# Capped attention and a gated MLP on one core: all four output projections after the gate stages, as seven block products for two batches at a time

## The chip, the cores and the metric

The kernel runs on one core of a Trainium2 chip. The metric is the device time of one execution in microseconds (us), as the median of several runs. The core has a matrix engine (PE, which multiplies a 128-row weight tile with up to 512 columns), and four others that compute or move data: DVE, ACT, POOL and SP. In this kernel SP issues nearly all transfers between DRAM and the on-chip memory SBUF; PE's results land in eight banks of PSUM.

## The reference

```python
# q, k, v: 4 batches x 12 heads x 448 positions x 64
scores = matmul(q, k.T) / sqrt(64)
scores = cap * tanh(scores / cap)              # cap = 30
scores = scores - max(scores, axis=-1)
attn = exp(scores)
attn = attn / (sum(attn, axis=-1) + 1e-9)
x = matmul(attn, v)                            # laid out as 1792 tokens x 768
g = x @ w_gate                                 # 768 -> 1536
val = x @ w_val                                # 768 -> 1536
return (g * sigmoid(g) * val) @ w_out          # 1536 -> 768
```

All of it is fp32. The 1792 tokens are 4 batches of 448.

## The kernel before

Every large product of fp32 operands is made of three products of a shorter format, fp32r: an operand is cast to fp32r (the high part, `wh`, `xh`), and the remainder, the operand less its high part, is kept as a second tile (`wl`, `xl`). High x high, low x high and high x low are added in PSUM (L924 to L926). So one block of 128 weight rows, 128 outputs and 448 columns costs three matmuls; an **atom** is two such blocks, six matmuls.

**Attention** works in pairs of heads; batch g has six pairs, u = 6g to 6g+5. A pair's scores are computed in four tiles of 112 keys (`qk`, L730, bank `sc`), tanh and exp follow on ACT (`t`, L737 and L740), DVE adds the four tiles (`total`, L744), PE multiplies with the values (`av`, L760), and a matmul against ones gives the denominators (`sm`). These come in two forms. In the two-tile form (L777) the sums are spread over 64 rows, 448 columns, and one reciprocal of 128x448 follows (L797). In the four-tile form (`spread`, L771), used in five pairs of batch 1, the sums lie on 32 rows each and 224 columns, the reciprocal is 128x224 (L783), and the result goes through DRAM (a small store and a load) to be spread over the rows. Then `x` = `av` x reciprocal (L801).

**Stages.** The head (to about 70 us) is the attention of batch 0, with the weights' first loads and their narrowing: each weight arrives as 64-bit pairs, is cut to fp32 (`wf`), and stored to DRAM for the later batches. Then follow, on PE: the gate stage of batch 0 (72 atoms, tiles k = 0 to 11, each with a gate half and a value half), between whose atoms the pairs of batch 1 stand; the output projection of batch 0 (k = 12 to 17, 36 atoms, from the gated features `hx`, kept in SBUF as high and low parts); the gate stage of batch 1 (k = 18 to 29), with the twelve pairs of batches 2 and 3; the output projection of batch 1; the **window**, the gate stage of batches 2 and 3 together; and their output projection. The last two stages use a 2x2 block scheme with seven block products instead of eight: tokens and weights are split in two halves each, sums and differences of blocks are formed on DVE (`blocks`, `comb`, `combos`), cast into the tiles `X1` to `X7`, and seven products p = 1 to 7 (the table `PROD`) are added in banks `b1` to `b3`. The window has 12 steps of seven products (`step`, L459 to L461), the outputs three times seven (`outs`, L637 to L639).

**What sets the order.** The class `Plan` is a list scheduler that runs when the kernel is built. Each piece of work is an operation with a priority (a planned time), the engines that may do it with an assumed duration, the operations that it needs and the buffers that it takes (`BUFS` gives their number). It places operation after operation, chooses an engine where several are allowed, and the resulting static order is emitted. `join` glues parts to one operation of PE: the value product, the sums and the first half of the next pair's scores. Pools of SBUF and PSUM are opened where their first tile is taken; by `TAKES` a pool takes over the room of another, and then waits until that is closed: `X` (all seven kinds) that of the attention pool `A`, `R` (`xr`, the attention results of batches 2 and 3) that of the narrowing pool `W`, `C` (`cc`, copies of PSUM banks) that of `R`.

In the gate stages, each weight half (128 x 768) is loaded, cast (`wH`, on ACT, DVE or POOL), and its remainder subtracted (`wL`, on DVE or POOL):

```python
op(("wL", k, half), tw - LEAD['wL'] * dt, {"POOL": 2.04, "DVE": 0.95}, wL, [("wH", k, half)], [("wl", atoms[-1:])])
```

Of the kernel before, what the change touches and what calls it, by code (L numbers as in the profile page):

```python
# [16 lines left out]
P = 128  # L17
C = 112
S = 448
B = 4  # L20
# [19 lines left out]
PACE = 26.0  # L40
# [5 lines left out]
JOIN = 7  # L46

# [3 lines left out]
    xr=12, X1=3, X2=3, X3=3, X4=3, X5=3, X6=3, X7=3, cc=7, hh=3, ss=3, b1=2, b2=2, b3=2,  # L51
    rq=2, rk=2, qh=1, ql=1, kh=1, kl=1, rv=2, t=8, s=2, r1=1, r=2, x32=2, xh=7, xl=7,
    w64=3, lo=2, wf=5, wh=4, wl=4, th=2, hx=12, o=2, sc=2, av=1, sm=1, mm=2,
# [5 lines left out]
    A="rq rk qh ql kh kl rv t r1 r x32 xh xl", X="X1 X2 X3 X4 X5 X6 X7", W="w64 lo", R="xr", C="cc hh",  # L59
    att="sc av sm", win="b1 b2 b3", sb="wf wh wl th hx o ss", mm="mm", total="s",  # L60
)
POOL_OF = {tag: name for name, tags in POOLS.items() for tag in tags.split()}
TAKES = {"X": "A", "R": "W", "C": "R", "win": "att"}


class Plan:
# [14 lines left out]
    def __init__(self, bufs):  # L81
        self.bufs = bufs
        self.ops = {}
        self.alias = {}

# [5 lines left out]
    def join(self, parts, save):  # L91

        head = self.ops[parts[0]]
        rest = [self.ops.pop(k) for k in parts[1:]]
        (engine, us), = head["where"].items()
        fns = [head["fn"]] + [o["fn"] for o in rest]
        head["where"] = {engine: us + sum(o["where"][engine] for o in rest) - save}
        head["fn"] = lambda e: [f(e) for f in fns]
        for o in rest:
            head["deps"] += o["deps"]  # L100
            head["alloc"] += o["alloc"]
        for k in parts[1:]:
            self.alias[k] = parts[0]

    def run(self):
# [8 lines left out]
        for o in ops.values():  # L114
            deps = [self.alias.get(d, d) for d in o["deps"]]
            o["deps"] = [d for d in dict.fromkeys(deps) if d != o["key"]]
            o["alloc"] = [(t, [self.alias.get(r, r) for r in rs]) for t, rs in o["alloc"]]
        users, nleft = {}, {}
        for k, o in ops.items():
            o["deps"] = [d for d in o["deps"] if d is not None]  # L120
            nleft[k] = len(o["deps"])
            for d in o["deps"]:
                users.setdefault(d, []).append(k)
# [13 lines left out]
        ready = {}  # L137

# [25 lines left out]
        alone = {"rec", "x", "ga", "va", "ov"}  # L164

        def shares(k, e):
            return e == "POOL" or e == "DVE" and k[0] not in alone
# [5 lines left out]
        while ready:  # L173
# [29 lines left out]
            else:  # L203
                free[e] = s + d
                end[k] = s + d
                if shares(k, e):
                    port = max(port, s + d)
            eng[k] = e
            for tag, readers in o["alloc"]:
# [15 lines left out]
def tile_capped_attention_gated_mlp(ctx: ExitStack, tc: tile.TileContext, qd, kd, vd, cap, eye, w1, w2, out):  # L225
# [7 lines left out]
    def pool(tag):  # L233
        name = POOL_OF[tag]
        if name not in opened:
# [4 lines left out]
            side = "right" if name in ("W", "R", "C", "att", "win") else "left"  # L240
# [3 lines left out]
    for tag in ("wf", "t", "w64", "mm", "sc"):  # L244
        pool(tag)
# [22 lines left out]


# [6 lines left out]
    total = [const.tile([P, 2, S], F32, name=f"total{i}") for i in range(BUFS["s"])]  # L276
# [30 lines left out]
    gcols = [S] * B  # L307
    GROUPS = [[(g, 0, NJ)] for g in range(B)]
    NG = B
# [9 lines left out]
    t += 0.5 * PAIR  # L319
    for g in range(2):  # L320
        L1, L2 = 72 * mm_us + 7.0 * (4 if g == 0 else 12), 36 * mm_us + 7.0 * (2 if g == 0 else 0)
        for a in range(108):
            z, L = (a / 72, L1) if a < 72 else ((a - 72) / 36, L2)
            atom_at[18 * g + a // 6, a % 6] = t + (L1 if a >= 72 else 0.0) + L * z
            atom_len[18 * g + a // 6, a % 6] = L / (72 if a < 72 else 36)
        if g == 0:
            for c in range(NCC):
                pair_at[NCC + c] = t + 2.0 + PACE * c
            for c in range(2 * NCC):
                pair_at[2 * NCC + c] = t + L1 + L2 - 4.0 + (72 * mm_us + 7.0 * 12 + 4.0) / (2 * NCC) * c  # L330
        else:
            split_at = t + L1 + 8.0
            combo_at = t + 0.5 * L1
        t += L1 + L2
    win_at = [t + 10.6 * mm_us * f for f in range(NFC)]
    t += 10.6 * mm_us * NFC
# [15 lines left out]
    for c in range(HALF):  # L352
        RAW[2, c] = [("XL", "B11", c), ("T1", c)]
        RAW[3, c] = [("XL", "T1", c)]
        RAW[2, c + HALF] = [("XL", "B21", c), ("T4", c)]
        RAW[3, c + HALF] = [("XL", "B22", c), ("T3", c), ("T2", c)]

    def blocks():
        def raw(z, c):
            return {  # L360
                "B11": ("x32", 2 * NCC + c), "B21": ("x32", 2 * NCC + c + HALF), "B12": ("x32", 3 * NCC + c),
                "B22": ("x32", 3 * NCC + c + HALF), "T1": ("x32", 3 * NCC + c),
            }.get(z, (z, c))

        def diff(e, z, a, b, c):
            if z != "T1":
# [3 lines left out]
        for c in range(HALF):  # L370
            t0 = split_at + 14.0 * c
            x = [("x", 2 * NCC + c), ("x", 2 * NCC + c + HALF), ("x", 3 * NCC + c), ("x", 3 * NCC + c + HALF)]
            n = 0
            for z, a, b, deps in (
                ("T3", "B22", "B12", x), ("T1", "B12", "B11", x + [("T3", c)]), ("T2", "B22", "T1", [("T1", c)]), ("T4", "B21", "T2", [("T2", c)]),
# [3 lines left out]
                   [("ss", users)] if z != "T1" else [])  # L379
                n += 1.5  # L380
        for n, z in enumerate(BLOCKS):
            p = next(p for p in PROD if PROD[p][3] == z)
            for c in range(HALF):
# [10 lines left out]
                order = split_at + 14.0 * c + 1.5 * n  # L394
# [4 lines left out]
    def step(f):  # L399
# [30 lines left out]
        def wL(e, n):  # L430
            T["wl", "w", f, n] = st([P, 6, P], F32R, "wl")[:, : 6 if n < 3 else 3]
            sub(e, T["wl", "w", f, n], source(n), T["wh", "w", f, n])

# [9 lines left out]
        for n in range(4):  # L443
# [4 lines left out]
            op(key("wL", n), tw + 1.0, {"DVE": 0.95 * k, "POOL": 2.04 * k}, lambda e, n=n: wL(e, n), [key("wH", n)], [("wl", [("p", f, last[n])])])  # L448
# [17 lines left out]
        prev = ("p", f - 1, 4) if f else ("mm", 35, 5)  # L466
# [6 lines left out]
        def keep(e, name, bank):  # L473
            T["cc", f, name] = st([P, S], F32, "cc")
# [7 lines left out]
        op(("c1", f), t0 + dt, both, lambda e: keep(e, 0, "b2"), [("p", f, 1)], [("cc", [("ga", "w", f, 0)])])  # L482
        op(("c11", f), t0 + 2 * dt, {"DVE": 0.62}, lambda e: plus(0, "b1"), [("p", f, 2), ("c1", f)])
        op(("cu", f), t0 + 3 * dt, both, lambda e: keep(e, 1, "b2"), [("p", f, 6)], [("cc", [("ga", "w", f, 1)])])
# [651 lines left out]
```

## Time and profile before

| | |
|---|---|
| median of 3 runs | 695.65 us (695.4 to 696.19) |
| the profiled execution | 696.79 us, of which the span of its instructions is 695.0 |
| busy: PE, DVE, ACT, POOL | 676.9 (97%), 566.7 (82%), 376.7 (54%), 100.8 us (14%) |
| mean DMA rate | 155 GB/s |

The span goes from the first to the last instruction of the execution; what lies around it is start and end of the program. Busy time counts what an engine computes, not its waiting or its issuing of transfers. PE's weight loads are a row of their own (PEld) and run beside its matmuls. The durations of matmuls overlap in the profile, so that their sum says less than their starts. A group of instructions is named by line, engine, operation and tiles: `mm<-hx,wl` is a matmul into `mm` from `hx` and `wl`.

### The profile page before, as it was taken

The numbers are of one execution on the slowest core, as the hardware profiler recorded it, in microseconds if no ns is written. First come the engines' busy times: TensorE is split into PE (matmuls) and PEld (weight loads), VectorE is DVE, ScalarE is ACT, GpSimd is POOL, SyncE is SP. The second block draws the span as 40 slices with busy tenths as digits, with TensorE's granted clock in tenths as the row PEclk, the third lists the DMA queues.
The fourth block names the chain that finished last, engine by engine and source line by source line (L and its number), as shares of the span: only waits on it lengthen the run. The fifth ranks groups of instructions, "written<-read, shape, count | busy, mean of one in ns | idle before, by whom it ended". The sixth has DMA issues, their size and how long they took to land.

```text
span 695.0 us, 9189 instructions
## 1 busy us (share of the span) xinstructions
PE 676.9 (97%) x3424; PEld 524.7 (75%) x3424; DVE 566.7 (82%) x694; ACT 376.7 (54%) x513; POOL 100.8 (14%) x86
## 2 busy tenths in 40 slices
PE   7889999999999999999999999999999999999996
PEld 2223787867867877777666777989999999989995
DVE  4999998999989577797997976988788798899740
ACT  6989667686765455454554653743433333474310
POOL 1312201021131022022220101002112111110000
PEclk9999999999999999999999999999999999999999
DMA  8655677896887533346784212131212212135311
GB/s 286 216 174 194 215 261 265 250 308 236 263 279 250 169 106 110 96 155 235 232 306 157 88 58 82 64 127 46 91 45 59 79 45 70 47 115 174 114 66 58
DMA packets 42652, 107.62 MB, mean 155 GB/s; under 512 B 4692, under 2 KB 19944, under 8 KB 42600
## 3 DMA queue, kind: packets, MB, share of 16 engines
q1 hardware_dynamic: 42312, 106.73, 46.4%
q8 instruction: 29, 0.48, 0.3%
q10 hardware_dynamic: 288, 0.23, 0.1%
q14 instruction: 23, 0.19, 0.1%
HBM read 82.54 MB, written 24.40 MB: 154 GB/s over the span
## 4 chain that ended last, share of the span: by engine, by line
PE 89%; DVE 6%; ACT 3%; DMA 1%; issue 0%; ACTq 0%; DVEq 0%
PE mm L924 14%; PE mm L925 13%; PE mm L926 13%; PE av L760 9%; PE sc L730 8%; PE b L459 7%; PE b L460 7%; PE b L461 7%; PE b L639 3%; PE b L638 3%; PE b L637 3%; DVE total L744 2%; PE sm L777 2%; ACT t L737 1%; DVE r L797 1%; ACT t L740 1%
## 5 line engine op out<-in xcount | busy, mean ns | idle before, releaser
L737 ACT ACTIVATE t<-sc 112x896 f32<-112x896 f32 x96 | 83.3, 917 | 71.2 <-PE sc L730 71.0
L267 DVE TENSOR_TENSOR wl<-wf,wh 128x768 fp32r<-128x768 f32 (+1 forms) x104 | 104.2, 1009 | 5.5 <-ACT wh L258 4.4
L924 PE MATMUL mm<-xh,wh 128*128 128x448 f32 x288 | 108.4, 377 | 0.0
L925 PE MATMUL mm<-xh,wl 128*128 128x448 f32 x288 | 105.3, 366 | 0.0
L926 PE MATMUL mm<-xl,wh 128*128 128x448 f32 x288 | 105.3, 365 | 0.0
L258 ACT ACTIVATE wh<-wf 128x768 fp32r<-128x768 f32 (+1 forms) x86 | 68.7, 799 | 64.7 <-PE b L639 14.7
L459 PE MATMUL b<-X,wh 128*128 128x448 f32 x252 | 92.2, 366 | 1.4 <-ACT cc L258 1.4
L460 PE MATMUL b<-X,wl 128*128 128x448 f32 x252 | 92.1, 365 | 0.0
L461 PE MATMUL b<-X,wh 128*128 128x448 f32 x252 | 92.1, 365 | 0.0
L740 ACT ACTIVATE t<-t 112x896 f32<-112x896 f32 x96 | 86.7, 955 | 0.1
L760 PE MATMUL av<-t,rv 112*64 112x448 f32 x384 | 77.5, 545 | 4.5 <-DVE x L801 4.3
L797 DVE RECIPROCAL r<-sm 128x448 f32<-128x448 f32 x19 | 56.2, 2956 | 24.2 <-PE sm L777 24.2
L924 PEld LDWEIGHTS mm<-xh,wh 128*128 128x128 f32 x288 | 54.1, 188 | 17.1 <-issue 11.9
L760 PEld LDWEIGHTS av<-t,rv 112*64 112x64 f32 x384 | 25.4, 136 | 48.1 <-issue 37.2
L926 PEld LDWEIGHTS mm<-xl,wh 128*128 128x128 f32 x288 | 54.1, 188 | 4.3
L925 PEld LDWEIGHTS mm<-xh,wl 128*128 128x128 f32 x288 | 54.2, 188 | 4.0 <-DVE wl L267 0.2
L744 DVE TENSOR_TENSOR total<-total,t 112x896 f32<-112x896 f32 x47 | 53.7, 1143 | 2.3 <-ACT t L740 2.1
L924 PE MATMUL mm<-hx,wh 128*128 128x448 f32 x144 | 53.7, 373 | 0.0
L926 PE MATMUL mm<-hx,wh 128*128 128x448 f32 x144 | 52.8, 366 | 0.0
L925 PE MATMUL mm<-hx,wl 128*128 128x448 f32 x144 | 52.7, 366 | 0.0
L459 PEld LDWEIGHTS b<-X,wh 128*128 128x128 f32 x252 | 47.4, 188 | 5.5 <-ACT cc L258 1.8
L461 PEld LDWEIGHTS b<-X,wh 128*128 128x128 f32 x252 | 47.4, 188 | 3.7
(121 smaller groups left out, 1164.7 us busy)
## 6 DMA issues: line engine op xcount, KB each, us to landing
wf<-w SPq DMA_DIRECT2D x81, 384.0 KB, 3.2
w<-w SPq DMA_DIRECT2D x36, 768.0 KB, 5.7
w<-wf SPq DMA_DIRECT2D x36, 384.0 KB, 4.1
rq<-qd SPq DMA_DIRECT2D x24, 224.0 KB, 4.5
rv<-vd SPq DMA_DIRECT2D x24, 224.0 KB, 3.1
rk<-kd SPq DMA_DIRECT2D x23, 224.0 KB, 4.7
w_S<-wf SPq DMA_DIRECT2D x12, 384.0 KB, 2.8
wf<-w_S SPq DMA_DIRECT2D x12, 384.0 KB, 3.2
```

The costliest lines, as they stand in the source:

```text
L258: nc.scalar.activation(out_, in_, AF.Copy, scale=1.0 if scale is None else scale)
L267: ENG[e].tensor_tensor(out_, a, b, op=ALU.subtract)
L459: nc.tensor.matmul(o, lhsT=wh, rhs=xh, start=first, stop=False, skip_group_check=True)
L460: nc.tensor.matmul(o, lhsT=wl, rhs=xh, start=False, stop=False, skip_group_check=True)
L461: nc.tensor.matmul(o, lhsT=wh, rhs=xl, start=False, stop=end, skip_group_check=True)
L737: nc.scalar.activation(T["t", u, j], T["sc", u, j][:C, :, :S], AF.Tanh, scale=icapr)
L740: nc.scalar.activation(T["t", u, j], T["t", u, j], AF.Exp, scale=capr)
L744: ENG[e].tensor_tensor(z, T["t", u, 0] if j == 1 else z, T["t", u, j], op=ALU.add)
L760: nc.tensor.matmul(T["av", u][D * i : D * i + D, :S], lhsT=T["rv", u][:C, i, j * D : j * D + D], rhs=T["t", u, j][:, i], start=j == 0, sto ...
L924: nc.tensor.matmul(o, lhsT=wh, rhs=xh, start=beg, stop=False)
L925: nc.tensor.matmul(o, lhsT=wl, rhs=xh, start=False, stop=False)
L926: nc.tensor.matmul(o, lhsT=wh, rhs=xl, start=False, stop=fin)
```

## The change

- **Outputs.** The two output projections of batches 0 and 1 (k = 12 to 17 and 30 to 35) are gone from their places. The gated features of these batches are stored to DRAM by SP (`hst`, 24 stores of 224 KB), and after the outputs of batches 2 and 3 (`outs(0)`) those of batches 0 and 1 follow in the same seven-product form (`outs(1)`), 378 matmuls where there were 432. Their features are loaded back (`hld`, 12 loads), planned 40 us ahead, into four slot kinds `H11` to `H22`, which batches 2 and 3 have used before. The w_out weights are loaded and cast a second time for `outs(1)`.
- **Narrowing of w_out** (12 halves) moves from batch 0's output stage into batch 1's gate stage, one tile every 20 us.
- **Denominators.** Pairs 6 to 22, without 11, use the four-tile form; they hold `av` in a copy in SBUF (`xk`, on ACT or DVE), which frees the bank, and multiply that copy in place when the reciprocals have come back.
- **Scores ahead.** For the pairs in `EARLY` the first half of the next pair's scores stands several products before the value product of the current one, and the second half directly before it, joined with it. The pairs of batches 2 and 3 run in the order c, c+3 of batch 2, then of batch 3 (`SEQ`).
- **Weight remainders.** For twelve halves of batch 1's gate stage (`FAR_1`: the gate halves of k = 18 to 29) the remainder is made otherwise: ACT writes -`wh` into `wl`, and a transfer issued by POOL adds `wf` to it in SBUF (`add_far`).
- **Pools.** Only `X3`, `X4`, `X5` take the attention pool's room; `X1`, `X2`, `X6`, `X7` take that of the narrowing; `cc`, `o` and `hx` are gone (`xr` tiles serve for the first two), `xr` is open from the start, `wf` has six buffers, `th` four, and the difference `T4` is made in place.

```diff
+FAR_1 = {(k, 0) for k in range(18, 30)}
+NARROW = 20.0
+GATES = {5,11,23}
+SPREAD = set(range(6,24)) - GATES
+HELD = set(range(6,24)) - GATES
+SEQ = list(range(2 * NCC)) + [NCC * g + c + h for c in range(NCC // 2) for g in (2, 3) for h in (0, NCC // 2)]
+NEXT = {u: z for u, z in zip(SEQ, SEQ[1:])}
+EARLY = set(SEQ[JOIN + 1 :]) - {2 * NCC}
-    A="rq rk qh ql kh kl rv t r1 r x32 xh xl", X="X1 X2 X3 X4 X5 X6 X7", W="w64 lo", R="xr", C="cc hh",
+    A="rq rk qh ql kh kl rv t r1 r x32 xh xl", X="X3 X4 X5", R="xr", W="w64 lo", Y="X1 X2 X6 X7", H="H11 H21 H12 H22 hh",
-TAKES = {"X": "A", "R": "W", "C": "R", "win": "att"}
+TAKES = {"X": "A", "Y": "W", "win": "att"}
...
+    def add_far(out_, in_):
+        flat = lambda z: z.rearrange("p a b -> p (a b)") if len(z.shape) == 3 else z
+        nc.gpsimd.dma_start(flat(out_), flat(in_), accum_op=ALU.add)
+
+    def rest(key, at, far, deps, fin, source, width=6, lead=5.0):
...
+        if not far:
+            op(("wL",) + key, at, {"POOL": 2.04 * k, "DVE": 0.95 * k}, lambda e: sub(e, new(), source(), T[("wh",) + key]), deps, [("wl", fin)])
+            return
+        op(("wN",) + key, at - lead, {"ACT": 0.85 * k}, lambda e: copy(e, new(), T[("wh",) + key], -1.0), deps, [("wl", fin)])
+        op(("wA",) + key, at - lead + 0.1, {"POOL": 0.86}, lambda e: add_far(T[("wl",) + key], source()), [("wN",) + key])
...
+    def outs(pr):
+        base = out_at + pr * len(OUT_ORDER) * 3 * mm_us
+        batches = (2, 3) if pr == 0 else (0, 1)
...
+        def hload(e, i, b, c):
+            T["h", pr, c + HALF * i, b] = st([P, 2, S], F32, f"H{i + 1}{b + 1}")
+            nc.sync.dma_start(T["h", pr, c + HALF * i, b], scratch["h", batches[b], c + HALF * i])
...
+                    op(("hld", i, b, c), base - 40.0 + 4.0 * i + 6.0 * b + c, {"SP": 1.28}, lambda e, i=i, b=b, c=c: hload(e, i, b, c),
+                       [("hst", g, z), ("hst", g, z + 1)], [hslot(pr, i, b, c)])
...
+            z = t0 + 3.8 * (j // 2)
+            if u in EARLY:
+                z = t0 - AHEAD if j < 2 else t0
...
+        def keep(e):
+            T["x32", u] = st([P, S], F32, "xr" if g else "x32")
+            copy(e, T["x32", u], T["av", u][:, :S])
...
-            op(("wL", k, half), tw - LEAD['wL'] * dt, {"POOL": 2.04, "DVE": 0.95}, wL, [("wH", k, half)], [("wl", atoms[-1:])])
+            rest((k, half), tw - LEAD['wL'] * dt, (k, half) in FAR_1, [("wH", k, half)], atoms[-1:], lambda half=half: T["wf", k, half])
...
+        def hst(e):
+            if i % 2 == 0:
+                scratch["h", g, i // 2] = dram.tile([P, 2, S], F32, name=f"hidden_{g}_{i // 2}")
+            nc.sync.dma_start(scratch["h", g, i // 2][:, i % 2], T["th", k])
...
-    outs()
+    outs(0)
+    outs(1)
     for u in range(JOIN, NU):
-        plan.join([("av", u), ("sum", u)] + ([("qk", u + 1, 0), ("qk", u + 1, 1)] if (u + 1) % NCC else []), 0.2)
+        nxt = NEXT.get(u)
+        if u in GATES:
+            plan.join([("av", u), ("sum", u)], 0.2)
+        elif nxt in EARLY:
+            plan.join([("qk", nxt, 2), ("qk", nxt, 3), ("av", u), ("sum", u)], 0.2, pair_at[nxt])
+            plan.join([("qk", nxt, 0), ("qk", nxt, 1)], 0.0)
+        else:
+            plan.join([("av", u), ("sum", u), ("qk", nxt, 0), ("qk", nxt, 1)], 0.2)
```

How the order changes is shown at three places. First PE, in the middle of batch 1's gate stage, around one attention pair; before:

```order
L926 MATMUL mm<-xl,wh 128x448
L760 MATMUL av<-t,rv 64x448 x8
L777 MATMUL sm<-total_81,ones 64x448 x2
L730 MATMUL sc<-qh,kl 112x448 x2
L730 MATMUL sc<-qh,kh 112x448 x2
L730 MATMUL sc<-ql,kh 112x448 x2
...
L924 MATMUL mm<-xh,wh 128x448
```

And now:

```order
L989 MATMUL mm<-xl,wh 128x448
L790 MATMUL sc<-qh,kl 112x448 x2
L790 MATMUL sc<-qh,kh 112x448 x2
L790 MATMUL sc<-ql,kh 112x448 x2
...
L822 MATMUL av<-t,rv 64x448 x8
L833 MATMUL sm<-total_85,ones 32x224 x4
L987 MATMUL mm<-xh,wh 128x448
```

The value product was followed by the sums and by the first two score tiles of the next pair; now the last two score tiles of the next pair stand directly before it, and the sums have the four-tile form.

Second ACT, around the window's first product, whose result stands in bank `b2` (`cc` or `xr` receives its copy). Before:

```order
L258 ACTIVATE wh_4081<-ss_4057 128x768
L258 ACTIVATE X5_4093<-xr_3513 128x448
L258 ACTIVATE o_4118<-mm_4040 128x448
L258 ACTIVATE wh_4122<-wf_3752 128x384
L258 ACTIVATE X6_4126<-ss_4120 128x448
L258 ACTIVATE wh_4143<-wf_4090 128x768
L258 ACTIVATE cc_4152<-b2_4108 128x448
```

And now:

```order
L1002 ACTIVATE th_3490<-mm_3448 128x448
L284 ACTIVATE X5_3531<-xr_2245 128x448
L284 ACTIVATE X5_3536<-xr_2766 128x448
L284 ACTIVATE X5_3539<-xr_3270 128x448
L284 ACTIVATE X3_3553<-xr_2383 128x448
L284 ACTIVATE X3_3556<-xr_2913 128x448
L284 ACTIVATE X3_3558<-xr_3368 128x448
L284 ACTIVATE xr_3561<-b2_3515 128x448
```

The copy of the first product stood behind a weight cast; now six casts into `X5` and `X3` stand directly before it, and those behind it follow.

Third POOL, in batch 1's gate stage, where `DMA wl<-wf` is an accumulating transfer. Before:

```order
L267 TENSOR_TENSOR wl<-wf,wh 128x768
L260 TENSOR_SCALAR wf<-w_1769 128x768
L267 TENSOR_TENSOR ql<-rq,qh 128x448
L267 TENSOR_TENSOR wl<-wf,wh 128x768
L260 TENSOR_SCALAR wh<-wf 128x768 x2
```

And now:

```order
L293 TENSOR_TENSOR kl<-rk,kh 128x448
L297 DMA wl<-wf 128x768
L286 TENSOR_SCALAR wh<-wf 128x768
L297 DMA wl<-wf 128x768
L286 TENSOR_SCALAR qh<-rq 128x448
L286 TENSOR_SCALAR wf<-w_1578 128x768
L297 DMA wl<-wf 128x768
L286 TENSOR_SCALAR qh<-rq 128x448
L804 TENSOR_TENSOR total_85<-total_85,t 112x896
L286 TENSOR_SCALAR wf<-w_1853 128x768
L297 DMA wl<-wf 128x768
```

POOL's own subtractions of weights have given way to casts, issued transfers and sums of score tiles.

## Rows read from the trace of the kernel before

**Rows 1.** The page: its head, the engines, the granted clock in 40 slices.

```profile
span 695.0 us, 9189 instructions
...
PE 676.9 (97%) x3424; PEld 524.7 (75%) x3424; DVE 566.7 (82%) x694; ACT 376.7 (54%) x513; POOL 100.8 (14%) x86
...
PEclk9999999999999999999999999999999999999999
```

**Rows 2.** Table by stage: length, busy PE, PEld, DVE, ACT, POOL, clock, DMA share, GB/s.

```profile
0.00:70.00 70.00, 59.84 (x274) 21.48 (x276) 60.23 (x64) 58.54 (x72) 15.24 (x16) 1.00 0.64 218
70.00:188.00 118.00, 118.00 (x596) 92.61 (x593) 109.48 (x138) 84.20 (x111) 16.24 (x12) 1.00 0.76 257
...
243.00:402.00 159.00, 159.00 (x874) 112.49 (x872) 131.92 (x148) 86.29 (x112) 29.90 (x27) 1.00 0.50 162
...
458.00:611.00 153.00, 151.59 (x749) 140.21 (x748) 126.70 (x178) 60.81 (x100) 27.46 (x23) 1.00 0.23 72
611.00:688.70 77.70, 77.44 (x375) 69.92 (x373) 51.90 (x59) 28.94 (x39) 1.32 (x1) 1.00 0.32 106
```

**Rows 3.** Waits of PE: us in total, times, longest us.

```profile
PE av L760 <- DVE x L801: 4.3, 4, 1.5
...
PE b L459 <- ACT cc L258: 1.4, 1, 1.4
...
PE mm L638 <- DVE wl L267: 0.3, 1, 0.3
```

**Rows 4.** The page's groups: busy us, mean ns; an output product of batches 0, 1.

```profile
L925 PE MATMUL mm<-hx,wl 128*128 128x448 f32 x144 | 52.7, 366 | 0.0
```

**Rows 5.** Timeline of PE: start us, length us; window stage, then last outputs.

```profile
500.11 0.36 PE L459 MATMUL b<-X,wh 128*128 128x448 f32 x1
...
502.54 0.36 PE L459 MATMUL b<-X,wh 128*128 128x448 f32 x1
...
685.47 0.37 PE L637 MATMUL b<-X,wh 128*128 128x448 f32 x1
...
688.37 0.37 PE L639 MATMUL b<-X,wh 128*128 128x448 f32 x1
```

**Rows 6.** Chain of waits: start us, length us; a four-tile and a two-tile pair.

```profile
113.59 3.16 PE av L760 x16
...
117.26 1.69 PE sc L730 x8
118.95 0.40 PE mm L924
119.35 0.20 PE mm L925
...
264.97 3.16 PE av L760 x16
...
268.88 1.40 PE sc L730 x12
```

**Rows 7.** Timeline of ACT at the window's start; then a group of it.

```profile
459.15 0.84 ACT L258 ACTIVATE wh<-wf 128x768 fp32r<-128x768 f32 x1 [2.30 <-issue]
459.90 0.53 ACT L258 ACTIVATE cc<-b 128x448 f32<-128x448 f32 x1
...
L258 ACT ACTIVATE X<-xr 128x448 fp32r<-128x448 f32 x12 | 6.4, 565 | 0.5 <-DVE xr L801 0.5
```

**Rows 8.** Groups of DVE by form: busy us, mean ns.

```profile
L797 DVE RECIPROCAL r<-sm 128x448 f32<-128x448 f32 x19 | 56.2, 2956 | 24.2 <-PE sm L777 24.2
...
L267 DVE TENSOR_TENSOR X<-hx,X 128x896 fp32r<-128x896 f32 x18 | 19.2, 1086 | 0.0
...
L783 DVE RECIPROCAL r<-sm 128x224 f32<-128x224 f32 x5 | 7.7, 1549 | 0.0
```

**Rows 9.** The page's DMA issues: KB each, us to landing.

```profile
wf<-w SPq DMA_DIRECT2D x81, 384.0 KB, 3.2
```

**Rows 10.** Timeline of ACT: the last copy of the kernel.

```profile
688.82 0.54 ACT L258 ACTIVATE o<-b 128x448 f32<-128x448 f32 x1 [3.22 <-PE b L639]
```

More of the change, by code (lines that the diff above doesn't have):

```diff
@@ L89, in op, with join @@
         self.ops[key] = dict(key=key, prio=prio + self.SHIFT.get(key[0], 0.0), where=where, fn=fn, deps=list(deps), alloc=list(alloc))
[L91 to L103, printed above, removed]
+    def join(self, parts, save, prio=None):
+        ops = [self.ops.pop(k) for k in parts]
+        key = ("join",) + parts[0]
+        (engine, _), = ops[0]["where"].items()
+        at = 0.0
+        for o in ops:
+            at += o["where"][engine]
+            self.part[o["key"]] = key, at
+        self.ops[key] = dict(
+            key=key, prio=ops[0]["prio"] if prio is None else prio, where={engine: at - save}, fn=lambda e: [o["fn"](e) for o in ops],
+            deps=[d for o in ops for d in o["deps"]], alloc=[x for o in ops for x in o["alloc"]],
+        )
     def run(self):
@@ L115, in run @@
             deps = [self.alias.get(d, d) for d in o["deps"]]
[L116 removed]
+            o["deps"] = [d for d in dict.fromkeys(deps) if d is not None and self.part.get(d, (d,))[0] != o["key"]]
             o["alloc"] = [(t, [self.alias.get(r, r) for r in rs]) for t, rs in o["alloc"]]
@@ L161, in room @@
             return t
-        alone = {"rec", "x", "ga", "va", "ov"}
+        alone = {"rec", "x", "ga", "va", "ov", "wA"}
         def shares(k, e):
-            return e == "POOL" or e == "DVE" and k[0] not in alone
+            return k[0] not in alone and e in ("POOL", "DVE")
         port = 0.0
@@ L208, in run @@
             eng[k] = e
+            for z in inside.get(k, ()):
+                end[z], eng[z] = min(s + self.part[z][1], end[k]), e
             for tag, readers in o["alloc"]:
@@ L275, in tile_capped_attention_gated_mlp @@
     ones = const.tile([P, D], F32, name="ones")
-    total = [const.tile([P, 2, S], F32, name=f"total{i}") for i in range(BUFS["s"])]
+    total = [pool("t").tile([P, 2, S], F32, name=f"total{i}", bufs=1) for i in range(BUFS["s"])]
     capr = nc.scalar.alloc_register("capr")
@@ L663, in outs @@
             end = {p: at[p, d] + step_us for p in PROD}
-            op(("oc1", d), end[1], both, lambda e, d=d: keep(e, 0, 1, d), [("o", 1, d, 2)], [("cc", [("os11", d)])])
-            op(("oc11", d), end[2], {"DVE": 0.62}, lambda e, d=d: plus(0, 2, d), [("o", 2, d, 2), ("oc1", d)])
-            op(("os11", d), end[2] + 0.5, {"SP": 0.7}, lambda e, d=d: store(d, 0, T["oc", 0, d]), [("oc11", d)])
-            op(("ocu", d), end[6], both, lambda e, d=d: keep(e, 1, 1, d), [("o", 6, d, 2)], [("cc", [("os12", d)])])
@@ L668, in outs @@
[L668 to L672 removed]
+            o = lambda p, d=d: ("o", pr, p, d, 2)
@@ new lines, in outs @@
+            c = lambda z, d=d: (z, pr, d)
+            op(c("oc1"), end[1], both, lambda e, d=d: keep(e, 0, 1, d), [o(1)], [("xr", [c("os11")])])
+            op(c("oc11"), end[2], {"DVE": 0.62}, lambda e, d=d: plus(0, 2, d), [o(2), c("oc1")])
+            op(c("os11"), end[2] + 0.5, {"SP": 0.7}, lambda e, d=d: store(d, 0, T["oc", pr, 0, d]), [c("oc11")])
+            op(c("ocu"), end[6], both, lambda e, d=d: keep(e, 1, 1, d), [o(6)], [("xr", [c("os12")])])
+            op(c("oc5"), end[5], both, lambda e, d=d: keep(e, 2, 5, d), [o(5)], [("xr", [c("os22")])])
```

366 lines of the change are left out of this document (177 added, 189 removed).

## Prediction

> **What bounds the kernel now.** I read the page's head first: the matrix engine PE is busy 676.9 us of a span of 695.0, at the full granted clock (nines in every slice, 2.4 GHz) [rows 1]. Then the table by stage: from 70 us to the last product PE is never idle for long, while DVE, the next engine, is busy 109 of 118 us in the first gate stage, 132 of 159 in the second, 127 of 153 in the window, 52 of 78 in the last outputs [rows 2]. Then the waits of PE: 4.3 us for `x` of DVE, all in the first 70 us, and one stop of 1.4 us for a `cc` copy of ACT at the window's start; the rest is tenths [rows 3]. So a microsecond taken from PE after 70 us is a microsecond of the span, if DVE, ACT and the transfers keep up. PE's price is not the 0.366 us that a matmul is shown with [rows 4]: they overlap, and what counts is start to start. From 500.11 to 502.54 us stand 12 steps, 0.2025 us each [rows 5].
>
> **Fewer products.** The outputs of batches 0 and 1 are 144 matmuls in each of three groups [rows 4], 432 in all. As seven block products of 54 for both batches together they are 378. 54 x 0.2025 = **-10.9 us**, all on PE's path, since the stages lose no other work that PE waited for.
>
> **Four-tile sums.** Eleven more pairs form their denominators in the form with four tiles. In the trace the value product starts at 113.59 and the next scores at 117.26, 3.67 us later, with that form; with the two-tile form 264.97 to 268.88, 3.91 [rows 6]. 11 x 0.24 = **-2.6**. On DVE the reciprocal falls from 2.96 to 1.55 us [rows 8], 11 x 1.41 = 15.5 us, off the path. The price is a store and a load through DRAM for each; the SP queue carries 22 small stores and loads more, and the numerator now waits in SBUF (one 448-column copy each, 16 in all, about 0.55 us on ACT or DVE), so that the bank is free before the sums return. The load is followed by `x`, which in these stages is wanted only one batch later: hidden.
>
> **Scores ahead.** The same matmuls in another order. Of PE runs of gate products between attention pieces there are 38 instead of 39; each costs 0.2 us of switching (0.40 against 0.20 for the first step [rows 6]). But in twelve pairs the scores now stand directly before the value product, a change of number format that the trace never shows in that form. Nearest is the step into or out of a gate run, 0.1 to 0.2 us; at the least it is free. I take 0.1: 12 x 0.1 - 0.2 = **+1.0**, ends -0.2 and +2.4. What it gives is slack: the softmax of a pair gets a whole pair's time.
>
> **Window start.** Before, ACT stood 2.30 us in front of a `wh` that waited for a buffer, and the copy of the first product's bank, which PE needed, stood behind it [rows 7]. Now six casts of X5 and X3 stand before that copy, and they can start only when batch 1's last gate product is over, for their pool takes the room of the attention's. 6 x 0.565 + 0.53 [rows 7] plus about 0.25 for the signals is 4.2 us; PE needs it after two block products, 18 x 0.2025 = 3.65. The stop of 1.4 becomes about 0.5: **-0.9**, ends -1.4 and 0.
>
> **DVE, ACT, POOL, transfers: at nothing, because they fit.** DVE gives up 24 `hx` differences, 15.5 us of reciprocals, ten sums of four (nine net on DVE, now on POOL) and a dozen weight remainders; it takes on 18 more `X` differences, 9 more block differences of 1.09 us [rows 8] and 17 weight casts of half a microsecond. Summed with the trace's durations, group by group, the total stays within 2 us of the 566.7 [rows 1]. By stage: first gate stage about 110 of 116 us of PE's time, 95% (before 93% [rows 2], where PE did not wait); second 137 of 169; window 136 of 153; outputs of batches 2 and 3 about 72 of 77, 94%, where the second half's blocks and weights are prepared; last outputs 45 of 77. The cover is thin in two of them. The gated features' 24 stores and 12 loads are 11 MB beside 0.23 to 0.50 DMA share [rows 2], loads planned 40 us ahead; the twelve w2 conversions and their loads move into the second gate stage, where the share was 0.50.
>
> **New stops.** First, batches 0 and 1 now meet without an output stage between them. `xh` and `xl` have seven slots, so five of batch 1's six chunks can be cut only while batch 0's last tile is being multiplied. Some eleven DVE instructions of 0.4 to 1.0 us, 6 us together, must run in the 8 to 9 us before PE wants the last chunk (18 gate products, two groups of scores of 1.4 us, then the first chunks). It fits if DVE is not late; if it is late by 2 us, so is PE. Second, in several pairs only one atom (six products, 1.2 us) stands between the two halves of a pair's scores, which share two banks with ACT's tanh. Third, the step from window to outputs, where PE waited 0.3 us for `wl` [rows 3], has more DVE work now. Together **+1.5**, ends 0 and +4.
>
> **The step itself.** In the last outputs 14 steps from 685.47 to 688.37 take 0.207 us each, not 0.2025, at the same clock [rows 5]. Looking over the runs between stops, the step is one of these two from a run's beginning to its end, 0.207 in about a fifth of them, whichever stage it is. I can't tell which one the last run of now about 1,600 products gets. All fast: -1.8 against before (457 slow ones x 0.004); all slow: +4.6. I take 0, the mean as before.
>
> **The sum.** -10.9 - 2.6 + 1.0 - 0.9 + 1.5 = -11.9 us. The head, up to 66 us, has the same PE order and the same sums on DVE; the tail (last product at 688.37 [rows 5], a copy at 688.82 [rows 10], the store, the end at 695.0) is the same too. Span 695.0 - 11.9 = 683.1. The profiled execution took 696.79, 1.79 more than its span, and the median of the runs, 695.65, lies 1.14 below it: 683.1 + 1.79 - 1.14 = **683.7 us**.
>
> **Rivals.**
> - *The accumulating transfers are late (slower than before).* In the second gate stage twelve weight remainders are no longer a DVE difference: ACT writes -`wh`, and a DMA issued by POOL adds `wf` to it. No row shows a transfer from POOL. The code plans the copy 5 us ahead of the point that lay 4 atoms before the product; with 72 atoms in about 169 us that is some 14 us, 13 after the copy. The same 384 KB take 3.2 us from SP [rows 9], so there are 10 us to spare. From a landing time of about 14 us the twelve waits eat the 12 us gained; at 16 us it would be 12 x 3 = 36 us, 708. Behind a waiting POOL transfer also stand POOL's own casts and sums. Against it: POOL is busy 30 of 159 us there [rows 2], and if a DVE instruction held the transfer's issue, the longest is 2.96 us [rows 8], so 3.2 + 3.0 = 6.2. Chance 0.07. The Trainium skill (SBUF — State Buffer, the box on DVE blocking a GpSimd-issued DMA under SBUF's two sides) says that such a DMA's descriptors can't be written while DVE holds the shared port, and shows 620 ns becoming 3100, five times; applied to 3.2 us, my estimate by that page is 16 us and a time near 708. By the same page the block ends with the DVE instruction, and then the sum stays as it is. No run here shows either yet.
> - *DVE or ACT becomes the bound* in the stages at 94 and 95%, or at the meeting of the batches: 4 to 6 us of stops instead of 1.5, 686 to 688.5. For it: DVE is already at 93% and a `wl` was late once. Against: DVE's sum does not grow, and PE did not wait at 93%. Chance 0.13.
> - *The last run gets the slow step*: +4.6, about 688. Chance 0.15, as often as long runs do.
> - *The change doesn't do what it says.* The instruction order has the 378 products and no `hx` product, so this has no more than 0.01.
>
> **How the numbers follow.** The forecast, 681 to 686.5, has 0.62; slow step 0.15; DVE or ACT 0.13; late transfers 0.07; the rest is a better end (no new stop and a fast last run, 679 to 681) and the unforeseen. The low end, with every term at its good end, is 678.8; I leave that corner out. From 680 to 690 lie the forecast, the slow step and the DVE case. A measurement of this kernel can tell 0.2%, 1.4 us, from no change: faster 0.89, the same 0.03 (a middling late transfer), slower 0.08.
>
> **What would show it.** Right: PE's matmul groups at 378 per two batches, no `hx` product, PE's waits after 70 us still under 3 us in sum, span near 683; the stop at the window's start about half a microsecond, again for an ACT copy; twelve POOL transfers landing in 3 to 7 us. Wrong: PE waiting for `wl` from a DMA in the second gate stage; for `xl` of DVE at the first products of batch 1; for `wl` in the outputs of batches 2 and 3; products spaced 0.207 us through the last 150 us; a start of the gate stage later than 70 us.

## The result, and the profile after

The changed kernel takes 683.78 us in the median of 4 runs (683.35 to 684.76); the kernel before, on the same chip, 695.92. The ratio is 0.9825, with a 95% interval of 0.9806 to 0.9843. A second measurement, beside the experiments, gave 684.07 (683.65 to 686.84) and 0.9837 (0.9814 to 0.986). The profiled execution took 684.11 us, of which the span is 682.1, where before it was 695.0 [rows 1].

The page of the changed kernel, its head and its engines:

```profile
span 682.1 us, 9443 instructions
...
PE 664.3 (97%) x3414; PEld 513.4 (75%) x3414; DVE 569.5 (83%) x710; ACT 386.6 (57%) x522; POOL 130.8 (19%) x98
```

PE is as full as before (97%), with 12.6 us less to do. DVE's sum is 569.5 where it was 566.7, POOL has 30 us more. The table by stage (stretch, length, then busy time of PE, PEld, DVE, ACT, POOL, and the granted clock, the DMA share and GB/s), cut where PE goes from one stage to the next: gate stage of batch 0, of batch 1, window, outputs of batches 2 and 3, outputs of batches 0 and 1:

```profile
70.00:191.30 121.30, 121.30 (x616) 88.26 (x612) 113.03 (x128) 74.49 (x97) 32.03 (x21) 1.00 0.83 277
191.30:364.80 173.50, 173.10 (x1018) 120.12 (x1017) 146.15 (x196) 123.85 (x162) 51.96 (x39) 1.00 0.71 209
364.80:520.70 155.90, 155.85 (x762) 142.77 (x761) 134.70 (x191) 66.82 (x111) 27.81 (x22) 1.00 0.38 126
520.70:598.30 77.60, 77.56 (x380) 70.94 (x379) 71.46 (x81) 40.65 (x54) 1.23 (x1) 1.00 0.62 215
598.30:674.80 76.50, 76.48 (x375) 69.93 (x373) 44.08 (x53) 21.82 (x29) 0.00 (x0) 1.00 0.30 100
```

Beside [rows 2]: the two output stages of 55 and 56 us are gone, the outputs stand at the end as two stages of 77 us, and PE is busy in all of them to within half a microsecond. DVE fills 113 of 121, 146 of 173 and 71 of 78 us, and PE waits for it there only once; its waits (us in total, times, longest us) have one row after the head:

```profile
PE av L822 <- DVE x L871: 4.3, 4, 1.5
PE sc L790 <- ACT t L797: 3.2, 6, 1.5
...
PE sc L790 <- DVE kl L293: 0.4, 1, 0.4
```

The first two are the head's (of the first, [rows 3] have the same); the waits for `cc` at the window's start and for `wl` in the outputs have gone, and one of 0.4 us for `kl` is new.

**Where the 12.9 us of the span are.** Counted from the starts of PE's matmuls in the two traces, term by term beside the prediction's:

| term | predicted | measured | how measured |
|---|---|---|---|
| 54 products fewer | -10.9 | -10.9 | 54 x 0.2027 |
| four-tile sums, 11 pairs | -2.6 | -2.75 | 11 x (5.42 - 5.17), below |
| scores ahead | +1.0 | 0.0 | 5.45 us a pair of batch 1 in both orders; all pieces between gate products 147.9 us before, 145.6 now, which the row above and `kl` account for |
| stop at the window's start | -0.9 | -1.6 | 1.58 between two products before, none now |
| new stops | +1.5 | +0.5 | `kl`, 0.46 beyond the usual gap |
| the product step | 0 | +0.6 | the 11.9 us that the products' runs lost, less the terms above; the steps' own sums give +0.8 (2.9 us over 0.2027 each, before 2.1), and the `wl` wait of 0.3 went |
| head and tail | 0 | +1.25 | first product 0.25 later; last product to end 7.65 against 6.64 |
| sum | -11.9 | -12.9 | 682.1 - 695.0 |

So the forecast time of 683.7 was met by 0.1 us, and not each of its terms: PE's path came out 2.3 us shorter than forecast, and the head, the end, and the distance from span to median (+1.7 us instead of the +0.65 taken over from before) gave 2.3 us back. That the sum came so close is luck.

### The profile page after: what moved, and what is told of

The parts are those of the page before. It is cut to its first block, busy times and chain, and to the rows that moved or that the text cites. A ratio compares the mean times of both kernels' runs of the same rounds, so it can differ in the third digit from the quotient of the medians.

```text
span 682.1 us, 9443 instructions
## 1 busy us (share of the span) xinstructions
PE 664.3 (97%) x3414; PEld 513.4 (75%) x3414; DVE 569.5 (83%) x710; ACT 386.6 (57%) x522; POOL 130.8 (19%) x98
## 4 chain that ended last, share of the span: by engine, by line
PE 85%; DVE 6%; ACT 3%; DMA 3%; issue 1%; SPq 0%; POOL 0%; ACTq 0%; DVEq 0%; POOLq 0%
PE mm L987 9%; PE av L822 9%; PE mm L989 8%; PE mm L988 8%; PE sc L790 8%; PE b L696 7%; PE b L695 6%; PE b L694 6%; PE b L500 6%; PE b L501 6%; PE b L502 6%; DVE total L804 2%; ACT t L797 1%; DMA wf<-w 1%; DVE r L859 1%; ACT t L800 1%
## 5 line engine op out<-in xcount | busy, mean ns | idle before, releaser
L284 ACT ACTIVATE wh<-wf 128x768 fp32r<-128x768 f32 (+1 forms) x72 | 57.2, 796 | 76.7 <-PE b L696 23.4
L293 DVE TENSOR_TENSOR wl<-wf,wh 128x768 fp32r<-128x768 f32 (+1 forms) x93 | 89.5, 964 | 5.9 <-ACT wh L284 5.3
L500 PE MATMUL b<-X,wh 128*128 128x448 f32 x252 | 92.6, 367 | 0.1
L501 PE MATMUL b<-X,wl 128*128 128x448 f32 x252 | 92.5, 367 | 0.0
L502 PE MATMUL b<-X,wh 128*128 128x448 f32 x252 | 92.4, 367 | 0.0
L696 PE MATMUL b<-X,wh 128*128 128x448 f32 x216 | 79.4, 368 | 0.0
L695 PE MATMUL b<-X,wl 128*128 128x448 f32 x216 | 79.2, 366 | 0.0
L694 PE MATMUL b<-X,wh 128*128 128x448 f32 x216 | 79.1, 366 | 0.0
L284 ACT ACTIVATE xr<-b 128x448 f32<-128x448 f32 x60 | 32.7, 545 | 79.5 <-PE b L696 48.2
L804 DVE TENSOR_TENSOR total<-total,t 112x896 f32<-112x896 f32 x38 | 47.7, 1254 | 3.5 <-ACT t L800 3.4
```

The lines of the kernel that those rows point to most:

```text
L500: nc.tensor.matmul(o, lhsT=wh, rhs=xh, start=first, stop=False, skip_group_check=True)
L501: nc.tensor.matmul(o, lhsT=wl, rhs=xh, start=False, stop=False, skip_group_check=True)
L502: nc.tensor.matmul(o, lhsT=wh, rhs=xl, start=False, stop=end, skip_group_check=True)
L694: nc.tensor.matmul(o, lhsT=wh, rhs=xh, start=first, stop=False, skip_group_check=True)
L695: nc.tensor.matmul(o, lhsT=wl, rhs=xh, start=False, stop=False, skip_group_check=True)
L696: nc.tensor.matmul(o, lhsT=wh, rhs=xl, start=False, stop=end, skip_group_check=True)
```

## The experiments

Each is the changed kernel with one thing altered, unless its text says otherwise; the scheduler then plans anew, so that other work changes its place and engine too. Times are medians of 4 to 5 runs, in one case of 10 and in one a single run; the changed kernel stands at 683.8. The runs were made on several chips, where the kernel before took 695.8 to 697.4 us beside them, so a microsecond between two of these kernels is settled only where a trace shows it.

**1. The four-tile sums alone taken back**

```diff
-SPREAD = set(range(6,24)) - GATES
-HELD = set(range(6,24)) - GATES
+SPREAD = set(range(6,11))
+HELD = set(range(6,11))
```

> The changed kernel with the four-tile denominators only in the five pairs that had them before; the other eleven use the two-tile form, and their value products are not held in a copy. Theory A (the form is worth 5.42 - 5.17 = 0.25 us of PE per pair, and DVE's 11 x 1.41 us more are hidden): 11 x 0.25 = 2.75, 686.5 us. Theory B (DVE's 15.5 us more, 160 of 175 us in batch 1's gate stage, come onto the path): PE waits for DVE by 2 us or more in sum, 688.5 us or more.

Measured: 685.19 us (685.05 to 685.35), 1.4 us more. The chain of waits of this kernel and of the changed one at a pair of batches 2 and 3 (start, length):

```profile
234.05 3.16 PE av L822 x16
237.21 0.75 PE sm L839 x4
237.96 0.40 PE mm L987
```

```profile
224.06 3.16 PE av L822 x16
227.22 0.52 PE sm L833 x8
227.74 1.41 PE sc L790 x12
229.15 0.40 PE mm L987
```

From the value product to the first matmul behind the sums 3.91 us became 3.68 ([rows 6] have 3.91 and 3.67). With the scores in front a pair takes 5.42 and 5.17 us of PE; that holds in all eleven, so the 2.75 us of theory A are there. The time rose by less because this kernel's end is 0.9 us shorter (6.74 us from the last product, below) and its product step a little shorter; PE waited 0.9 us for a `kl` of DVE, not the 2 us or more of theory B. B's load did not come whole, either: DVE has 9 us more, not 15.5, and 156 us of work in the 176 of that stage.

**2. The accumulating transfers alone taken back**

```diff
-FAR_1 = {(k, 0) for k in range(18, 30)}
+FAR_1 = set()
```

> The changed kernel without accumulating transfers: the twelve weight remainders of batch 1's gate stage are subtracted on DVE again (97 of them in all instead of 85). Theory A (DVE has room: 144 of 172 us in that stage, 156 with the twelve): PE waits for nothing new, +0 to +1 us; and if the microsecond that the end of the program has grown by belongs to the queue of POOL's transfers, that goes: 682.8 to 684.5 us. Theory B (the transfers were needed, since what counts is the gate stage's dense places): PE waits for wl or kl of DVE, 3 us or more in sum, 687 us or more.

Measured: 684.84 us (684.7 to 685.08), 0.3 us outside theory A and far from B. A's "nothing new" was wrong: PE waits 1.3 us for `kl` (0.4 in the changed kernel) and 1.2 us for the copy at the window's start. Its end of the program came: that is 0.83 us shorter, and so the time rose by 1.1 only. In the changed kernel itself the transfers landed in time; the view of the line that issues them:

```profile
L297 POOL DMA_DIRECT2D wl<-wf x12: 863/878/1165, 185.7 to 348.8; - x12
...
DMA to landing us min/median/max: 3.9/7.1/9.7
```

The view names nobody who waited for them. Their 7.1 us is twice what SP's transfers of the same size, from DRAM, took in the kernel before [rows 9].

**3. The scores ahead taken back, and two kernels more on it**

```diff
-EARLY = set(SEQ[JOIN + 1 :]) - {2 * NCC}
+EARLY = set()
```

> The changed kernel without the scores ahead: the first two score tiles of the next pair stand behind the value product again, as before the change. Theory A (the order of the scores costs PE nothing and gives only slack that the other parts do not need, 5.45 us a pair in either order in batch 1): 683.3 to 684.8 us. Theory B (the slack is needed since the sums on DVE and POOL are later than before): PE waits for t of ACT or for total of DVE in several pairs, 2 us or more, 686 us or more.

Measured: 701.93 us (701.08 to 703.05), slower than before the change by a ratio of 1.0087 (1.0067 to 1.0106). Theory A fell. B's time came, but not by waits in several pairs: nearly all of them belong to the last pair and to the window's start. The waits of PE, and its timeline where the gate stage of batch 1 ends (start, length, instruction, and in brackets the idle time before it and what ended it):

```profile
PE b L500 <- issue: 3.8, 1, 3.8
PE b L500 <- DVE xr L520: 3.7, 1, 3.7
...
PE b L501 <- DVE wl L293: 0.9, 2, 0.6
```

```profile
327.32 3.23 PE L822 MATMUL av<-t,rv 112*64 112x448 f32 x16
...
341.52 3.23 PE L822 MATMUL av<-t,rv 112*64 112x448 f32 x16
...
355.68 3.23 PE L822 MATMUL av<-t,rv 112*64 112x448 f32 x16
...
361.23 0.45 PE L790 MATMUL sc<-qh,kl 64*112 64x448 f32 x2 [0.41 <-ACT t L797]
...
366.16 1.81 PE L822 MATMUL av<-t,rv 112*64 112x448 f32 x8 [1.48 <-ACT t L800]
368.49 0.97 PE L839 MATMUL sm<-total,ones 113*64 113x448 f32 x4 [0.51 <-DVE total L804]
373.23 0.48 PE L500 MATMUL b<-X,wh 128*128 128x448 f32 x1 [3.77 <-issue]
```

From value product to value product PE takes 14.2 us. Between the first two of them DVE ends the last sum of the next pair's tiles at 340.41:

```profile
339.33 1.08 DVE L804 TENSOR_TENSOR total<-total,t 112x896 f32<-112x896 f32 x1
```

In the changed kernel the value products stand closer:

```profile
305.40 3.23 PE L822 MATMUL av<-t,rv 112*64 112x448 f32 x16
...
318.42 3.23 PE L822 MATMUL av<-t,rv 112*64 112x448 f32 x16
...
331.38 3.23 PE L822 MATMUL av<-t,rv 112*64 112x448 f32 x16
...
340.11 3.23 PE L822 MATMUL av<-t,rv 112*64 112x448 f32 x16
```

13.0, 13.0 and 8.7 us, and 11.7 in the mean of all twelve, against 14.2. In the old order a pair's first scores stand behind the last pair's value product, and two rounds of tanh and exp on ACT and the sums on DVE follow before its own: from 327.32 to 340.41 that is 13.1 of the 14.2 us. Twelve pairs at that pace are 12 x 14.2 = 170 us, which is all of batch 1's gate stage with its 72 atoms (173.5 in the changed kernel). Before the change batch 1's output products gave them cover: the last value product stood at 426 us, in the second of the two output stages that [rows 2] leave out (402 to 458). With that stage gone, the last pair stands bare: after 359 us no gate product is left, PE waits for ACT, then 3.77 us, in which by the chain of waits DVE makes the last pair's reciprocal (2.97) and result, and the window starts with DVE behind (3.7 and 0.9 us more). The pace is that of this plan: whether another plan for the old order could keep gate products for the last pair was not tried. In the window's first 3.7 us the granted clock was 0.54, most of it at 1.2 GHz of the two levels 1.2 and 2.4, PE having stood before it:

```profile
373.20:376.90 3.70, 3.67 (x11) 3.33 (x12) 3.70 (x8) 3.61 (x8) 0.00 (x0) 0.54 0.00 0
376.90:380.00 3.10, 2.26 (x10) 1.50 (x8) 3.10 (x6) 2.45 (x5) 0.00 (x0) 1.00 0.00 0
```

Three kernels tell this apart from its rivals: that every stage hangs on the order, or that another part of the change needs it. In the first only batches 2 and 3 keep the scores ahead (`EARLY = set(SEQ[2 * NCC + 1 :])`):

> The changed kernel with the scores ahead only among batches 2 and 3's pairs; batch 1's pairs have the old order. Theory A (the order is needed where twelve pairs must fit beside 72 atoms, and not where six do): 682.8 to 685 us. Theory B (every pair needs it): a good part of e4_early0's 18 us, 688 us or more.

Measured: 683.71 us (683.48 to 684.03). Batch 1's pairs, six beside batch 0's 72 atoms, do not need it. In the second the outputs, the pools and the narrowing's place are all that is left of the change (`EARLY` and `FAR_1` empty, `SPREAD` and `HELD` as in 1):

> The changed kernel with the scores in their old order, with four-tile denominators in the old five pairs alone and without accumulating transfers: what is left of the change are the outputs at the end, the store and load of the features, the narrowing's new place and the pools. Theory A (a pair needs some 14 us of its own where its scores stand behind the last value product, and twelve of them do not fit beside 72 atoms once the output stage has gone): as e4_early0, 700 to 708 us, with the last pairs uncovered ahead of the window. Theory B (it was the holding of the value products or the pools that made e4_early0 slow): 690 us or less.

Measured: 701.2 us (699.75 to 701.72), ratio 1.0063 (1.0044 to 1.0083). The 54 products saved are lost again, and more. So the holding of the value products is not the cause; the pools are still in this kernel, and the next clears them too. It has the outputs and the scores ahead, and neither transfers nor four-tile sums:

> The changed kernel with the outputs at the end and the scores ahead, but without accumulating transfers and with four-tile denominators in the old five pairs alone: the two parts that the other runs left as carrying the gain. DVE does 11 + 15 us more than in the changed kernel, which in batch 1's gate stage comes to about 170 of 178 us. Theory A (the parts add: e2_far0 cost 1.0 us and e3_two_tile 1.4): 685.5 to 687 us. Theory B (at 95% DVE becomes the bound): PE waits for DVE by several us, 688.5 us or more.

Measured: 686.7 us (686.47 to 686.94), ratio 0.986 (0.9843 to 0.9876). The parts add (683.8 + 1.0 + 1.4 = 686.2), and in this plan the scores ahead are worth 701.2 - 686.7 = 14.5 us to the change, 14.1 by the two ratios. Theory B was not put to its test: DVE has 13 us more than in the changed kernel (582.8), not 26, and 160 of the stage's 176 us.

**4. The product step**

In the changed kernel's window the step changes within every window step, always at the same products. Their tiles gave the lead: `X1`, `X2`, `X6`, `X7`, the right-hand pools, lie at odd multiples of 32 bytes in SBUF, `X3` to `X5` at multiples of 64 (as the pools are laid out; the trace shows no addresses). An unused tile of 32 bytes moves the right-hand ones:

```diff
+    pad = ctx.enter_context(tc.tile_pool(name="pad", bufs=1, side="right"))
+    pad.tile([P, 8], F32, name="pad8")
     for tag in ("wf", "t", "xr", "w64", "mm", "sc"):
```

> The changed kernel with one unused tile of 32 bytes ahead of the right-hand pools of SBUF, so that every X tile starts at a multiple of 64 bytes; nothing else moves. Theory A (the longer step, 0.2067 us instead of 0.2027, belongs to products whose moving tiles all lie at an odd multiple of 32 bytes, as X1, X2, X6 and X7 do in the changed kernel): the 561 long steps from 344 us on go, 561 x 0.004 = 2.2 us, with the half microsecond of the mixed steps between them up to 2.8: 681.0 to 681.6 us. Theory B (the step is set by where PE stood at the last stop, whatever the addresses): the steps are the one or the other from stop to stop, and the time stays within 1 us of 683.8, or rises by up to 4 us where long runs get the longer one.

Measured: 682.88 us (681.36 to 684.19), runs at 681.4, 681.6, 684.1 and 684.2. The timeline of PE at the same place, in the changed kernel and in this (24 and 25 steps from the first row to the last):

```profile
378.10 0.36 PE L502 MATMUL b<-X,wh 128*128 128x448 f32 x1
...
383.06 0.37 PE L502 MATMUL b<-X,wh 128*128 128x448 f32 x1
```

```profile
377.96 0.37 PE L502 MATMUL b<-X,wh 128*128 128x448 f32 x1
...
383.02 0.36 PE L503 MATMUL b<-X,wl 128*128 128x448 f32 x1
```

4.96 / 24 = 0.2067 and 5.06 / 25 = 0.2024 us. From 365 us to the last product the changed kernel's 1,506 recorded steps are 2.7 us longer than at 0.2027 each (in both of its profiles, with more than a third of them long), this one's 0.0. But two of its runs were as long as before, and of those there is no profile. The same kernel once more:

> e1_align once more, for one more profile. If its time is near 684.2 us, theory A (POOL's sum meets ql) expects a wait of PE for kl of 2 to 3 us at some 240 us and short steps everywhere, theory B (the step) no such wait and long steps in the window or the outputs; if it is near 681.4, both expect its first profile again.

It took 681.85 us, with no long step from 314 us on again, so this told nothing of the upper runs. The changed kernel was run again too:

> The changed kernel again, beside e7_mix. Its long steps are tied to addresses, so they come in every run alike: 683.4 to 684.8 us, the window and the outputs with the same long stretches as in its first profile.

The steps came as expected, in the same places; the times did not, two of five being 686.7 and 686.8, and for those there is no profile. Two more kernels told more. In one, half of `X5` lies 32 bytes off (mixed addresses in one product group), in the other the sums of score tiles are taken from POOL:

> As e1_align, all right-hand tiles at multiples of 64 bytes, but the low half of each X5 tile lies 32 bytes off its high half, so that one product of each of the window's steps, and two in each output part, mixes both kinds of address. Theory A (where all tiles are at multiples of 64 the step stays as the last stop left it, 0.2027 or 0.2067, as e1_align's runs of 681.4 and 684.2 and the kernel before show; a mixed product brings it back to 0.2027 at once): every run near 681.4 us, none above 682.5. Theory B (the two times of e1_align have another cause): runs at 681.4 and at 684.2 again.

Measured: 684.11 us (682.46 to 684.83); theory A fell, long steps are back (some 25 in a row in each 126 of the window). Its profile, of 684.83 us, has a second cause as well, in the timeline of DVE and POOL; the changed kernel's below it:

```profile
237.83 0.92 POOL L304 DMA_DIRECT2D wl<-wf  x1
...
238.03 3.34 DVE L300 TENSOR_TENSOR ql<-rq,qh 128x448 fp32r<-128x448 f32 x1 [1.45 <-POOL qh L293]
238.45 2.42 POOL L812 TENSOR_TENSOR total<-total,t 112x896 f32<-112x896 f32 x1
...
241.29 0.61 DVE L300 TENSOR_TENSOR kl<-rk,kh 128x448 fp32r<-128x448 f32 x1
```

```profile
236.33 0.63 DVE L293 TENSOR_TENSOR ql<-rq,qh 128x448 fp32r<-128x448 f32 x1 [1.34 <-POOL qh L286]
236.86 2.39 POOL L804 TENSOR_TENSOR total<-total,t 112x896 f32<-112x896 f32 x1
236.88 2.87 DVE L293 TENSOR_TENSOR kl<-rk,kh 128x448 fp32r<-128x448 f32 x1
...
239.90 0.46 PE L790 MATMUL sc<-qh,kl 64*112 64x448 f32 x2 [0.40 <-DVE kl L293]
```

A sum on POOL that meets DVE's remainder holds it from 0.62 to 3.34 or 2.87 us: it ends half a microsecond behind POOL's. Where it is `kl` that is held, PE waits 0.2 to 0.4 us; where it is `ql`, one place earlier, `kl` comes behind it and PE waits 2.6. By the Trainium skill (SBUF — State Buffer, "SBUF: two separate sides") a DVE operation with two inputs in SBUF and a GpSimd operation that reads SBUF take one port pair as an exclusive lock, and the one that starts second waits for the end of the first. That the remainder ends just behind the sum agrees. Who starts first agrees in one row only: `kl` starts 0.02 us behind the sum, but `ql` 0.42 us ahead of it, while POOL still issues a transfer (the first row above). The next kernel has the transfers and not the sums.

> As e1_align, and from the seventh pair on the sums of score tiles are made on DVE alone, not on POOL (ten fewer on POOL, 10 x 1.08 = 11 us more on DVE). Theory A (a POOL sum that meets DVE's ql or kl at 237 us holds that instruction from 0.6 to 2.9 or 3.3 us; where it hits kl, PE waits 0.2 to 0.4 us, where it hits ql, kl comes behind it and PE waits 2.6 us, as in e7_mix; this is the distance of 2.5 to 3 us between the low and the high runs): the two levels become one, near 681.4 us, if DVE has room for the 11 us. Theory B (the two levels are those of the step): runs at 681.4 and 684.2 stay. Theory C (DVE has no room): PE waits for DVE's sums, 683.5 us or more.

Measured: 682.06 us (681.83 to 685.31), ratio 0.9789 (0.9771 to 0.9807). No wait for `kl` is left, and no `ql` or `kl` takes over 0.8 us, so the sums, not the transfers, are what holds them. DVE is busy 574.7 us, 4 more than in e1_align and not 11, and has room for that; theory C fell. But two of five runs are still 2.5 to 3.3 us up. (This ratio lies below the changed kernel's, but the interval meets that of its first measurement; which of these kernels is best is not settled by it.) The profile is of the longest. Its steps at 440 and at 600 us, 24 and 25 from row to row:

```profile
439.67 0.36 PE L504 MATMUL b<-X,wh 128*128 128x448 f32 x1
...
444.54 0.36 PE L504 MATMUL b<-X,wh 128*128 128x448 f32 x1
...
599.80 0.37 PE L696 MATMUL b<-X,wh 128*128 128x448 f32 x1
...
604.97 0.37 PE L697 MATMUL b<-X,wl 128*128 128x448 f32 x1
```

4.87 / 24 = 0.2029 before a stop of 0.1 us at 465.4, and 5.17 / 25 = 0.2068 behind it, to the end: 1,011 long steps, 4.0 us. For this run theory B holds. And the other way round, in the kernel before:

> The kernel before, with 32 unused bytes ahead of the X tiles, so that all of them lie at odd multiples of 32 bytes; nothing else moves. Theory A (such products always take the longer step): all 1,134 products from 458 us on at 0.2067, where the window's 756 took 0.2027: 756 x 0.004 = 3.0 us more, 698.5 to 699 us. Theory B (a step is set at a stop, not by addresses): 695.7 us, within 1.5 us.

Measured: 696.21 us (695.57 to 696.6, 10 runs), ratio 0.9989 (0.998 to 0.9998). Theory A as worded fell: tiles at odd multiples of 32 bytes do not make a step long. Its steps in the window and in the outputs, 25 and 26 from row to row, lie between and below the two:

```profile
559.77 0.37 PE L463 MATMUL b<-X,wh 128*128 128x448 f32 x1
...
564.88 0.36 PE L461 MATMUL b<-X,wh 128*128 128x448 f32 x1
...
639.76 0.36 PE L639 MATMUL b<-X,wh 128*128 128x448 f32 x1
...
644.96 0.36 PE L641 MATMUL b<-X,wh 128*128 128x448 f32 x1
```

5.11 / 25 = 0.2044 and 5.20 / 26 = 0.2000 us. So over a stretch the step has at least four values; where all moving tiles have one kind of address it keeps one from stop to stop, and where the kinds are mixed it changes with the product. What picks the value at a stop stays open.

## Why the prediction was right, and where it was lucky

The time fell inside the range, and met the forecast by luck: several terms came out better than said, and the head, the end and what lies outside the span took it back.

**What bounds the kernel** was read rightly: PE after 70 us. Its path fell by what was taken from it, 10.9 us of products and 2.75 of sums (steps "Fewer products" and "Four-tile sums", right to 0.15 us).

**Scores ahead** is the step that failed, twice. Its price, +1.0, was nothing: the change of number format costs nothing in that order. And "what it gives is slack" left out for whom: that the output stage of batch 1 covered the last pairs of batches 2 and 3. The sentence that "the stages lose no other work that PE waited for" holds only with the scores ahead; without them, in this plan, the change is slower than before (701.2 and 701.9). The prediction looked for the cost of the move in DVE's share and in the meeting of the batches, and not in what now stands beside the last of twelve pairs; that this did not show is because the change carried its own remedy.

**Window start.** The mechanism was right, its size off: the six casts took 2.92 us, not 6 x 0.565, since they overlap. The copy ended as PE came to need it:

```profile
365.00 2.92 ACT L284 ACTIVATE X<-xr 128x448 fp32r<-128x448 f32 x6 [3.10 <-PE mm L989]
367.82 0.52 ACT L284 ACTIVATE xr<-b 128x448 f32<-128x448 f32 x1
```

The copy is over at 368.35; PE, 18 products from 364.80, needs it at 368.5. The stop of 1.6 us went whole, by a margin of a tenth. In the kernel of experiment 2 the plan puts nine casts there, and PE waits its 1.2 us behind them:

```profile
365.86 4.32 ACT L284 ACTIVATE X<-xr 128x448 fp32r<-128x448 f32 x9 [2.16 <-DMA wf<-w]
370.09 0.52 ACT L284 ACTIVATE xr<-b 128x448 f32<-128x448 f32 x1
```

**DVE, ACT, POOL and transfers fit**, as said: DVE at 569.5 against 566.7 (2.8 us up, where within 2 was said), the stages at 93, 84, 86, 92 and 58%, and with 13 us more on it (experiment 3, last kernel) the parts still add. No stop stood at the meeting of batches 0 and 1, and none of the reloads was waited for.

**New stops** were put at three places, and none there was longer than 0.2 us; the one that came, `kl` behind a POOL sum, was not among them.

**The accumulating transfers** landed in 3.9 to 9.7 us, against 3 to 7 forecast, inside the 13 us behind the copy that it had worked out. The rival by the Trainium skill (SBUF — State Buffer, the same section), 16 us and 708, did not come: DVE was busy 146 of 174 us beside them, and no transfer took 10. Its sum was off as well: 12 x 3 = 36 us on 683.7 are 720, not 708.

**The step** was taken at its old mean, with "all fast" and "all slow" as ends; it was neither, 0.8 us worse by the steps' own sums, with the tiles' addresses mixed, which the trace of before does not show.

**The end** was said to be the same, and is a microsecond longer.

## What to carry to other kernels

When a stage is moved, list what stood beside it as well as what it costs: here the output products that were saved had been the cover of the last attention pairs, and in this plan only the reordering of the scores made the saving real. A forecast that meets the time can do so with errors that cancel; check it term by term, from the starts of the bounding engine. A sum given to POOL is not free while DVE does two-input work (0.62 us became 2.87 and 3.34 here): look where the two meet, one place ahead of what PE needs.

## What the hardware showed

- The distance from start to start of a full product (128x128, 448 columns, full clock) took 0.2000, 0.2027, 0.2044 or 0.2067 us, as the mean of stretches of hundreds of products. It changed at a stop (once at one of 0.1 us), and within the window's steps where the tiles' addresses are of two kinds modulo 64 bytes.
- The end of the program, from the last product's start, took 7.5 to 7.7 us in eight of nine profiles of kernels with transfers issued by POOL (6.74 in the ninth), and 6.4 to 6.8 in the five without. What in the end takes the microsecond was not tried.
- An accumulating transfer of 384 KB within SBUF took 3.9 to 9.7 us from its issue on POOL.
